# Softmax sums from a column of ones in the stage ahead of the expert slots

## The chip, the cores and the metric

One NeuronCore of one Trainium2 chip runs the whole program. The metric is the device time of one execution in microseconds (us), the median of the runs shown; differences are of a few us in some 650.

## The reference

Windowed attention, whose output rows are then sent through a mixture of eight experts, one expert for each token:

```
q, k, v: (8, 8, 576, 64) float32         # batch, heads, sequence, head_dim
scores = q k^T / 8, only where 0 <= i - j < 64, else -1e9
scores -= max;  attn = exp(scores);  attn /= (sum(attn) + 1e-9)
x = (attn v) as (4608, 512)              # token rows, heads side by side
logits = x w_gate + modality_bias[modality_id];  e_idx = argmax(logits)
gate_w = the chosen expert's softmax probability
out[rows of e] = gate_w * (relu(x w1[e]) w2[e])   # w1: 512x1024, w2: 1024x512
```

## The kernel before, in words

The 4608 token rows are 36 pairs of two 64-row blocks, 128 rows each. A block of queries sees its own block of keys and the one before. The main loop (L947 on) has one step s for each pair, and four more; each step holds work of several pairs, one stage each: scores and minima of pair s, transposes of the probabilities of pair s-1, values of pair s-2, router logits of pair s-3. Two pairs form a group G, for which queries and keys are turned (transposed on TensorE, copied out of PSUM by `heads_out`) in the steps before: the keys in the even step, the queries in the odd one, each in two halves of four heads.

The order of the instructions on every engine is that of the program text (`manual_schedule`); no scheduler changes it. An engine works through its queue in order, and waits where the next instruction's input is not there.

In one step, for pair s: TensorE computes `scores` into two PSUM banks sp0 and sp1; VectorE takes the row minima of the negated, masked scores head by head (`minima`, tile ss, mn); ScalarE takes the exponentials head by head (`exps`) and with `accum_out` also their sums, read by an instruction of its own (ACTIVATION_READ_ACCUMULATOR); a step later TensorE turns the probabilities (`probs_t`) and ScalarE copies them to pT; GpSimd adds 1e-9 to the sums (`sums`, tile rs). The values come in as vo (128 rows, heads, 64). The keys of a row's window lie in its own block and the one before, so a second tile ve holds the values exchanged: GpSimd copies the pair's lower half into ve's lower rows and VectorE the neighbour pair's upper half into ve's upper rows (`swap_v`, L503 and L502; "the neighbour copy" below is the latter). `values` multiplies pT with ve and vo into one PSUM bank av, 32 matmuls in the trace's count of two for each product; `values_out` takes the reciprocal of rs and multiplies (tile xa). `x_t` turns xa, `logits` and `route1` to `route3` choose the expert and compute each row's place, and GpSimd scatters xa's rows to a scratch tensor in DRAM, sorted by expert (L716).

All turns ask `turn_bank` for a PSUM bank: before step 11 there are five (two of tp, and em, y0, y1, which the slots use later), from step 11 on the two of tp.

Beside that, expert weights come in as pieces of 128x512, which are split into a high part (ScalarE, L111) and a low part (VectorE, L116), one piece a step.

From step FIRST = 12 on, pieces of expert slots stand between the parts of a step: matmuls of 256 sorted rows with one expert's weights, in three products of high and low parts (L279, L301). After the last step only slots remain. A wait is chosen by the order: the first slot's rows are loaded in step 11 (`fetch`).

The names and lines that matter: `turn_bank` L474, `load_v` L483, `swap_v` L495, `heads_out` L534, `exps` L583, `sums` L601, `values` L607, `values_out` L619, and the step's body from L947.

Of the kernel before, what the change touches and what calls it, by code (L numbers as in the profile page):

```python
# [19 lines left out]
P = 128  # L20
W64 = 64
# [5 lines left out]
def tile_window_attn_moe(  # L27
# [447 lines left out]
    def turn_bank(s):  # L475

        i = n_tp[0]
        n_tp[0] += 1
        if s < FIRST - 1 and i % 5 > 1:
            return ps_m.tile([P, 512], F32, name=("em", "y0", "y1")[i % 5 - 2])  # L480
        return ps_t.tile([P, 512], F32, name="tp")

    def load_v(p):  # L483
        t = work.tile([P, H, D], F32, name="vo", bufs=3)
        vo[p] = t
        g0, g1 = 2 * p, 2 * p + 1
        if g0 // BPB == g1 // BPB:
            s0 = (g0 % BPB) * W64
            nc.sync.dma_start(out=t, in_=v_v[g0 // BPB, s0:s0 + P])
        else:  # L490
            for i, g in enumerate((g0, g1)):
                s0 = (g % BPB) * W64
                nc.sync.dma_start(out=t[i * W64:(i + 1) * W64], in_=v_v[g // BPB, s0:s0 + W64])

    def swap_v(p):  # L495

        e = work.tile([P, H, D], F32, name="ve", bufs=2)
        ve[p] = e
        if p == 0:
            nc.gpsimd.memset(e[W64:P], 0.0)  # L500
        else:
            nc.vector.tensor_copy(out=e[W64:P], in_=vo[p - 1][W64:P])  # L502
        nc.gpsimd.tensor_copy(out=e[0:W64], in_=vo[p][0:W64])  # L503

    def new_qk(G, nm):
        if G in AHEAD:
# [94 lines left out]
    def sums(p):  # L601
        sm = st[p, "s"][2]
        rs = st[p, "rs"] = small.tile([P, H], F32, name="rs")
        nc.gpsimd.tensor_scalar(out=rs, in0=sm, scalar1=1e-9, scalar2=None, op0=ALU.add)


    def values(p):  # L607
        st.pop((p, "s"))
        av = st[p, "av"] = ps_a.tile([P, H, D], F32, name="av")
        for u in range(H):  # L610
            a, hp = divmod(u, HP)
            pT = st[p, "p", a]
            for c in range(2):
                i = hp * P + c * W64
                nc.tensor.matmul(  # L615
                    out=av[c * W64:(c + 1) * W64, 2 * hp + a], lhsT=pT[:, i:i + W64],
                    rhs=(vo if c else ve)[p][:, 2 * hp + a, :], start=True, stop=True)

    def values_out(p):  # L619
        rs = st.pop((p, "rs"))  # L620
        nc.vector.reciprocal(out=rs, in_=rs)
        xa = st[p, "xa"] = xas[p % XBUF]
        nc.vector.tensor_tensor(  # L623
            out=xa[:, 0:DM].rearrange("p (h d) -> p h d", d=D), in0=st.pop((p, "av")),
            in1=rs[:, :, None].broadcast_to([P, H, D]), op=ALU.mult)
# [24 lines left out]
    def route1(G):  # L650

        lg = st.pop((G, "lg"))
        oh = chosen[G]
        lm = small.tile([P, GB], F32, name="lm")
        ex = small.tile(sh3, F32, name="ex")
        wn = small.tile(sh3, F32, name="wn")
        wm = small.tile([P, GB], F32, name="wm")
# [187 lines left out]
    for h in range(2):  # L845
        rows = slice(h * W64, (h + 1) * W64)
        own = slice(h * W64, (h + 1) * W64)
        before = slice((1 - h) * W64, (2 - h) * W64)
        for m in range(3):
            nc.gpsimd.affine_select(  # L850
                out=masks[rows, m, own], in_=masks[rows, m, own],
                compare_op=ALU.is_ge, fill=NEG, base=0,
                pattern=[[-1, W64]], channel_multiplier=1)
            if m == h + 1:
                nc.gpsimd.memset(masks[rows, m, before], NEG)
            else:
# [89 lines left out]
    for s in range(NPR + 4):  # L946
# [201 lines left out]
    while next(it, "end") != "end":  # L1148
# [6 lines left out]
        for n in range(RAWS):  # L1155
            if n < len(swaps) and n == len(ahead) and swaps[n][0] <= t + RAWS:
                _, buf, x, c = swaps[n]
                tick(ready_a - issued[0], table=True)
                nm = ("vo", "ss", "pT")[n_raw[0] % RAWS % 3]
                n_raw[0] += 1  # L1160
                sh = [P, H, D] if nm == "vo" else [P, HP, P] if nm == "ss" else [P, HP * P]
                raw = work.tile(sh, F32, name=nm, bufs=2 if nm == "pT" else 3)
                if nm != "pT":
                    raw = raw.rearrange("p a b -> p (a b)")
# [130 lines left out]
```

## Time and profile before

| what | us |
|---|---|
| median of three runs | 648.55 |
| lowest and highest | 647.55 and 649.33 |
| profiled execution | 648.28 |
| its span | 646.4 |
| busy in the span: TensorE | 620.0 |
| VectorE | 367.7 |
| ScalarE | 299.4 |
| GpSimd | 137.4 |

The profile shows one execution. Busy time of an engine is the time in which one of its instructions runs; of TensorE it is a modelled time, since matmuls overlap. Instructions on VectorE and ScalarE overlap a little too: the next one starts before the one ahead has written its last element, so what an instruction costs its engine is read from its start to the next one's start. "PE" is TensorE, "DVE" VectorE, "ACT" ScalarE, "POOL" GpSimd, "SP" the queue that starts most transfers. In the page's 40 slices of 16 us TensorE is at six to eight tenths in the first six, and at nine or more in nearly all that follow: the first part is the attention alone, steps 0 to 11, up to about 88 us.

### The profile page before, as it was taken

Reading aid. Unit: us, or ns where it says so; the run is one execution under the profiler, and the core shown is the slowest. Engines: PE = TensorE matmul, PEld = TensorE weight load, DVE = VectorE, ACT = ScalarE, POOL = GpSimd, SP = SyncE. Lnnn points to the kernel's source line nnn. Section 1 sums busy time; section 2 is a strip of 40 time slices with the busy share of each in tenths; the row PEclk is TensorE's granted clock in tenths of the full one; section 3 lists DMA queues with packets and bytes.
Section 4 is the critical chain, followed back from the end, with each engine's and each line's share of the span. In section 5 each row is a group of like instructions: output and inputs, shape, how many; then the busy total and the mean of one; then the engine's idle time right before and its main releaser. Section 6 shows DMA issues by size and latency. Waiting matters only on the chain.

```text
span 646.4 us, 17286 instructions
## 1 busy us (share of the span) xinstructions
PE 620.0 (96%) x6508; PEld 554.6 (86%) x6509; DVE 367.7 (57%) x1494; ACT 299.4 (46%) x932; POOL 137.4 (21%) x314
## 2 busy tenths in 40 slices
PE   6888889999999999999999999999999999999996
PEld 4677779898989888889998898899898999989986
DVE  2889967777767686766655365122214524757611
ACT  2789875756565646555544111111113513555411
POOL 4315330232142212320322220011011101101102
PEclk9999989999999999999999999999999999999999
DMA  9988975764876754553412124421041732677300
GB/s 164 195 186 216 212 197 132 196 161 120 181 171 153 159 144 103 144 133 82 132 51 83 50 99 171 157 67 66 23 173 45 236 113 85 218 247 227 120 1 36
DMA packets 138885, 88.07 MB, mean 136 GB/s; under 512 B 116746, under 2 KB 116784, under 8 KB 138672
## 3 DMA queue, kind: packets, MB, share of 16 engines
q1 hardware_dynamic: 130112, 67.44, 42.2%
q0 software_dynamic: 5856, 18.92, 7.8%
q10 hardware_dynamic: 2832, 0.59, 0.6%
q8 instruction: 52, 0.85, 0.6%
q14 instruction: 33, 0.27, 0.2%
HBM read 67.49 MB, written 23.91 MB: 141 GB/s over the span
## 4 chain that ended last, share of the span: by engine, by line
PE 50%; DVE 0%; ACT 0%; issue 0%; POOL 0%; POOLq 0%; ACTq 0%
PE y L301 22%; PE em L279 12%; PE sp L279 10%; PE tp L439 1%; PE y L352 1%; PE av L615 1%; PE em L254 1%; PE tp L254 1%; PE sp L327 0%; PE em L327 0%; PE tp L640 0%; PE sp L563 0%; DVE xa L623 0%; ACT ss L589 0%; DVE hl L288 0%
## 5 line engine op out<-in xcount | busy, mean ns | idle before, releaser
L301 PE MATMUL y<-Whi,hh 128*128 128x512 f32 x288 | 118.7, 412 | 0.0
L301 PE MATMUL y<-Wlo,hh 128*128 128x512 f32 x288 | 112.9, 392 | 0.0
L301 PE MATMUL y<-Whi,hl 128*128 128x512 f32 x288 | 112.8, 392 | 0.0
L589 ACT ACTIVATE ss<-ss,mn 128x128 f32<-128x128 f32 x288 | 112.5, 397 | 0.0
L279 PE MATMUL em<-xh,Whi 128*128 128x256 f32 x400 | 103.5, 293 | 1.2 <-ACT xh L192 0.7
L279 PE MATMUL em<-xh,Wlo 128*128 128x256 f32 x400 | 98.5, 280 | 0.0
L288 DVE SCALAR_TENSOR_TENSOR hl<-em,hh 128x512 fp32r<-128x512 f32 x50 | 34.5, 690 | 92.9 <-ACT hh L287 91.3
L312 POOL DMA_INDIRECT out_dram<-y,id x36 | 37.3, 1036 | 224.6 <-DVE y L309 145.9
L279 PEld LDWEIGHTS em<-xh,Whi 128*128 128x128 f32 x400 | 75.9, 190 | 2.6 <-ACT xh L192 0.9
L279 PEld LDWEIGHTS em<-xh,Wlo 128*128 128x128 f32 x400 | 75.8, 190 | 0.9
L287 ACT ACTIVATE hh<-em 128x512 fp32r<-128x512 f32 x50 | 29.6, 592 | 93.3 <-PE em L279 89.4
L577 DVE CUSTOM_DVE_ANT_0 ss<-sp,masks 128x128 f32<-128x128 f32 x288 | 63.5, 286 | 13.4 <-PE sp L563 13.4
L598 ACT COPY pT<-tp 128x512 f32<-128x512 f32 x58 | 32.2, 589 | 78.0 <-PE tp L439 78.0
L301 PEld LDWEIGHTS y<-Whi,hl 128*128 128x128 f32 x288 | 54.1, 188 | 12.3
L279 PE MATMUL em<-xl,Whi 128*128 128x256 f32 x400 | 63.4, 281 | 0.0
L301 PEld LDWEIGHTS y<-Whi,hh 128*128 128x128 f32 x288 | 54.1, 188 | 7.5
L301 PEld LDWEIGHTS y<-Wlo,hh 128*128 128x128 f32 x288 | 54.3, 188 | 7.1
L589 ACT ACTIVATION_READ_ACCUMULATOR ss<-ss,mn 128x1 f32 x288 | 55.8, 194 | 0.0
L716 POOL DMA_INDIRECT xs_scratch<-xa,idx x36 | 36.3, 1007 | 89.1 <-DVE lm L659 26.9
L279 PEld LDWEIGHTS em<-xl,Whi 128*128 128x128 f32 x400 | 54.2, 189 | 0.0
L288 DVE SCALAR_TENSOR_TENSOR hl<-sp,hh 128x512 fp32r<-128x512 f32 x22 | 15.2, 692 | 61.1 <-ACT hh L287 61.1
L615 PEld LDWEIGHTS av<-ve,pT 128*64 128x64 f32 x576 | 36.4, 138 | 15.2 <-issue 7.4
(242 smaller groups left out, 1243.6 us busy)
## 6 DMA issues: line engine op xcount, KB each, us to landing
xt<-xs_scratch SPq DMA_DIRECT2D x18, 514.0 KB, 4.0
vo<-in_v_dram SPq DMA_DIRECT2D x32, 256.0 KB, 4.1
y<-in_moe_w_dram SPq DMA_DIRECT2D x32, 256.0 KB, 4.0
vo<-in_moe_w_dram SPq DMA_DIRECT2D x24, 256.0 KB, 3.5
ss<-in_moe_w_dram SPq DMA_DIRECT2D x24, 256.0 KB, 3.8
qk<-in_k_dram SPq DMA_DIRECT2D x18, 256.0 KB, 5.5
qk<-in_q_dram SPq DMA_DIRECT2D x18, 256.0 KB, 4.9
xs_scratch<-xs_scratch SPq DMA_DIRECT2D x8, 514.0 KB, 6.0
```

The lines of the kernel that those rows point to most:

```text
L254: nc.tensor.transpose(out=tp[:, n * P:(n + 1) * P].bitcast(F32R), in_=xt[:, t, c * P:(c + 1) * P].bitcast(F32R), identity=ident_r)
L279: nc.tensor.matmul(out=hb[:, i * TP:(i + 1) * TP], lhsT=w[buf][:, c0:c0 + P], rhs=x[:, c * TP:(c + 1) * TP], start=(n == 0), stop=(n == le ...
L287: nc.scalar.activation(out=hh, in_=hb, func=AF.Relu),
L288: nc.vector.scalar_tensor_tensor(out=hl, in0=hb, scalar=0.0, in1=hh.bitcast(F32), op0=ALU.max, op1=ALU.subtract)))
L301: nc.tensor.matmul(out=sl["y", t], lhsT=h[:, i * TP + t * P:i * TP + (t + 1) * P], rhs=w[buf][:, c0:c0 + DM], start=(k == 0 and n == 0), s ...
L312: ins = nc.gpsimd.indirect_dma_start(out=out, out_offset=bass.IndirectOffsetOnAxis(ap=sl["id"][:, t:t + 1], axis=0), in_=y, in_offset=None ...
L352: nc.tensor.matmul(out=yp[:, cols], lhsT=sl["h", n][lo][:, c * P:(c + 1) * P], rhs=w[buf][:, c0 + cols.start:c0 + cols.stop], start=(m == ...
L577: nc.vector.tensor_tensor_reduce(out=ss[a][:, hp, :], in0=sp[a][:, hp * P:(hp + 1) * P], in1=mask, scale=-1.0 / 8.0, scalar=3.0e38, op0=AL ...
L589: nc.scalar.activation(out=ss[a][:, hp, :], in_=ss[a][:, hp, :], func=AF.Exp, bias=mn[:, h:h + 1], scale=-1.0, accum_out=sm[:, h:h + 1])
L598: nc.scalar.copy(out=pT, in_=pp)
L615: nc.tensor.matmul(out=av[c * W64:(c + 1) * W64, 2 * hp + a], lhsT=pT[:, i:i + W64], rhs=(vo if c else ve)[p][:, 2 * hp + a, :], start=Tru ...
L716: ins = nc.gpsimd.indirect_dma_start(out=xs, out_offset=bass.IndirectOffsetOnAxis(ap=idx[:, j:j + 1], axis=0), in_=xg[j], in_offset=None)
```

## The change

It concerns the pairs p < 12 (FIRST), whose work stands mostly ahead of the slots.

- The value tiles vo and ve get a 65th column for each head, set to one at the start. The exponentials no longer give sums (`accum_out` is None for p < 12). `values` takes 65 columns, so column 64 of each head's product is the sum of the probabilities. Eight heads of 65 columns don't fit one PSUM bank, so four heads go to av and four to y1.
- `values_out` adds 1e-9 to the two columns of sums on VectorE (two instructions of 128x4), takes the reciprocal as before, and multiplies in two parts of 128x256. GpSimd's add goes.
- `turn_bank` has four banks instead of five before step 11, without y1.
- The neighbour copy moves from VectorE, behind the minima, to ScalarE, at the start of the step (`swap_upper`). For p >= 12 it stays on VectorE, and also moves to the step's start.
- The second half of the queries' copy moves from VectorE to ScalarE in the steps before 12, as the second half of the keys' was.
- vo and ve become fixed tiles instead of ones drawn from a pool; two small tiles share names with others (wm with lm, tgt with wn).

```diff
-        if s < FIRST - 1 and i % 5 > 1:
-            return ps_m.tile([P, 512], F32, name=("em", "y0", "y1")[i % 5 - 2])
+        if s < FIRST - 1 and i % 4 > 1:
+            return ps_m.tile([P, 512], F32, name=("em", "y0")[i % 4 - 2])
...
     def swap_v(p):
-        e = work.tile([P, H, D], F32, name="ve", bufs=2)
-        ve[p] = e
+        e = ve[p]
         if p == 0:
             nc.gpsimd.memset(e[W64:P], 0.0)
-        else:
-            nc.vector.tensor_copy(out=e[W64:P], in_=vo[p - 1][W64:P])
         nc.gpsimd.tensor_copy(out=e[0:W64], in_=vo[p][0:W64])
+
+    def swap_upper(p):
+        ve[p] = ves[p % 2]
+        if p > 0:
+            copy = nc.scalar.copy if p < FIRST else nc.vector.tensor_copy
+            copy(out=ve[p][W64:P], in_=vo[p - 1][W64:P])
...
-                bias=mn[:, h:h + 1], scale=-1.0, accum_out=sm[:, h:h + 1])
+                bias=mn[:, h:h + 1], scale=-1.0, accum_out=sm[:, h:h + 1] if p >= FIRST else None)
...
-        av = st[p, "av"] = ps_a.tile([P, H, D], F32, name="av")
+        av = [ps_a.tile([P, 512], F32, name="av")]
+        if p < FIRST:
+            av.append(ps_m.tile([P, 512], F32, name="y1"))
+            av = [t[:, 0:HP * (D + 1)].rearrange("p (h d) -> p h d", h=HP) for t in av]
...
+        if p < FIRST:
+            for i in range(2):
+                nc.vector.tensor_scalar(
+                    out=rs[:, i * HP:(i + 1) * HP], in0=av[i][:, :, D], scalar1=1e-9, scalar2=None, op0=ALU.add)
         nc.vector.reciprocal(out=rs, in_=rs)
...
+        if 1 <= s <= NPR:
+            swap_upper(s - 1)
...
-            heads_out(tp, G, *heads[1], nc.scalar.copy if heads[1] == K1 else nc.vector.tensor_copy)
+            heads_out(tp, G, *heads[1], nc.scalar.copy if heads[1] == K1 or s < FIRST else nc.vector.tensor_copy)
```

On VectorE, in step 7 and the start of step 8 (ve is the neighbour copy's target, qT the queries', tgt or wn the rows' places, Wlo a weight piece, rs the sums, lg the logits), before:

```order
L502 COPY ve<-vo 64x512
L539 COPY qT<-tp 128x2x2x128
L697 TENSOR_TENSOR tgt<-tp,ebase 128x16
L539 COPY qT<-em 128x2x2x128
L702 TENSOR_REDUCE se<-ex 128x2
...
L116 TENSOR_TENSOR Wlo_66<-y,Whi_65 128x512
L621 RECIPROCAL rs<-rs 128x8
L623 TENSOR_TENSOR xa_102<-av,rs 128x512
L645 TENSOR_TENSOR lg<-y_1245,bias_sel 128x8
```

and after:

```order
L545 COPY qT<-tp 128x2x2x128
L720 TENSOR_TENSOR wn<-em,ebase 128x16
L725 TENSOR_REDUCE se<-ex 128x2
...
L116 TENSOR_TENSOR Wlo_66<-y,Whi_65 128x512
L641 TENSOR_SCALAR rs<-av 128x4
L641 TENSOR_SCALAR rs<-y_1239 128x4
L643 RECIPROCAL rs<-rs 128x8
L646 TENSOR_TENSOR xa_102<-av,rs 128x256
L646 TENSOR_TENSOR xa_102<-y_1239,rs 128x256
L668 TENSOR_TENSOR lg<-tp,bias_sel 128x8
```

Two copies are gone from the step; two adds and a second multiplication have come.

On ScalarE, in step 7 (Whi is a weight piece, pT the probabilities, xaT the turned rows, the exponentials are the ones on ss), before:

```order
L111 CAST Whi_65<-y 128x512
L598 COPY pT<-em 128x512
L598 COPY pT<-y_1161 128x512
L589 ACTIVATE ss,sm<-ss,mn 128x128 x2
L632 COPY xaT<-y_1172 128x512
L589 ACTIVATE ss,sm<-ss,mn 128x128 x6
L111 CAST Whi_65<-y 128x512
```

and after:

```order
L111 CAST Whi_65<-y 128x512
L509 COPY ve_110<-vo_109 64x520
L604 COPY pT<-em 128x512
L604 COPY pT<-y_1174 128x512
L595 ACTIVATE ss<-ss,mn 128x128 x2
L655 COPY xaT<-tp 128x512
L595 ACTIVATE ss<-ss,mn 128x128 x6
L545 COPY qT<-y_1212 128x2x2x128
L111 CAST Whi_65<-y 128x512
```

The neighbour copy stands ahead of the probabilities' copies, the second query copy behind the exponentials, and the exponentials write no sums.

## Rows read from the trace of the kernel before

**Rows 1.** Busy us (instructions) by stretch: PE, PEld, DVE, ACT, POOL; clock, DMA share, GB/s
```profile
60.00:75.00 15.00, 12.58 (x225) 11.02 (x225) 14.45 (x82) 14.33 (x55) 7.41 (x13) 1.00 0.96 219
...
105.00:120.00 15.00, 15.00 (x229) 13.24 (x228) 12.50 (x60) 9.19 (x31) 3.62 (x7) 1.00 0.52 138
```

**Rows 2.** Timeline of VectorE: start us, duration us, engine, line, operation [idle before <-releaser]
```profile
18.97 0.29 DVE L577 CUSTOM_DVE_ANT_0 ss<-sp,masks 128x128 f32<-128x128 f32 x1 [2.20 <-PE sp L563]
...
48.73 0.28 DVE L577 CUSTOM_DVE_ANT_0 ss<-sp,masks 128x128 f32<-128x128 f32 x1
...
56.47 0.42 DVE L502 COPY ve<-vo 64x512 f32<-64x512 f32 x1
56.93 0.69 DVE L539 COPY qT<-tp 128x512 f32<-128x512 f32 x1
...
57.74 0.68 DVE L539 COPY qT<-em 128x512 f32<-128x512 f32 x1
58.34 0.16 DVE L702 TENSOR_REDUCE se<-ex 128x2 f32<-128x16 f32 x1
...
58.88 0.15 DVE L728 CAST idx<-dst 128x2 int32<-128x2 f32 x1
...
59.54 0.20 DVE L621 RECIPROCAL rs<-rs 128x8 f32<-128x8 f32 x1
59.82 0.69 DVE L623 TENSOR_TENSOR xa<-av,rs 128x512 f32<-128x512 f32 x1
60.43 0.15 DVE L645 TENSOR_TENSOR lg<-y,bias_sel 128x8 f32<-128x8 f32 x1
60.50 0.28 DVE L577 CUSTOM_DVE_ANT_0 ss<-sp,masks 128x128 f32<-128x128 f32 x1
...
66.32 0.28 DVE L577 CUSTOM_DVE_ANT_0 ss<-sp,masks 128x128 f32<-128x128 f32 x1
...
83.46 0.69 DVE L539 COPY qT<-tp 128x512 f32<-128x512 f32 x1 [0.67 <-PE tp L439]
```

**Rows 3.** Waits from 15 to 95 us: engine, line, awaited: total us, times, longest us
```profile
DVE ss L577 <- PE sp L563: 4.0, 3, 2.2
```

**Rows 4.** Timeline of ScalarE, step 0 and steps 6 and 7
```profile
14.72 0.41 ACT L589 ACTIVATE ss<-ss,mn 128x128 f32<-128x128 f32 x1
...
17.81 0.60 ACT L539 COPY kT<-tp 128x512 f32<-128x512 f32 x1
...
49.06 0.59 ACT L598 COPY pT<-em 128x512 f32<-128x512 f32 x1
49.54 0.41 ACT L589 ACTIVATE ss<-ss,mn 128x128 f32<-128x128 f32 x1
49.85 0.20 ACT L589 ACTIVATION_READ_ACCUMULATOR ss<-ss,mn 128x1 f32 x1
...
51.96 0.21 ACT L663 ACTIVATE ex<-lg 128x16 f32<-128x16 f32 x1
52.06 0.39 ACT L589 ACTIVATE ss<-ss,mn 128x128 f32<-128x128 f32 x1
...
55.24 0.59 ACT L598 COPY pT<-em 128x512 f32<-128x512 f32 x1 [0.89 <-PE em L439]
```

**Rows 5.** Timeline of TensorE, steps 7, 8, 9 and 11
```profile
54.49 0.66 PE L439 MATMUL em<-ident_r,ss 128*128 128x128 f32 x4
...
59.65 0.66 PE L439 MATMUL y<-ident_r,ss 128*128 128x128 f32 x4
...
63.24 0.27 PE L615 MATMUL av<-ve,pT 128*64 128x64 f32 x1 [1.15 <-DVE lg L660]
...
79.41 0.65 PE L439 MATMUL tp<-ident_r,ss 128*128 128x128 f32 x4 [0.94 <-DVE lg L645]
```

**Rows 6.** Timeline of GpSimd: its half of ve behind two scatters
```profile
62.33 0.86 POOL L503 COPY ve<-vo 64x512 f32<-64x512 f32 x1
```

**Rows 7.** Busy us by stretch, columns as in the first group, at the first slot
```profile
92.00:94.00 2.00, 2.00 (x11) 2.00 (x11) 1.51 (x6) 0.86 (x5) 0.77 (x1) 0.50 0.64 182
```

More of the change, by code (lines that the diff above doesn't have):

```diff
@@ L459, in tile_window_attn_moe @@
     first_oh = small.tile([P, GB + 1, E], BF16, name="oh", bufs=3)
+    vos = [att.tile([P, H, D + 1], F32, name=f"vo{i}") for i in range(3)]
+    ves = [att.tile([P, H, D + 1], F32, name=f"ve{i}") for i in range(2)]
     v_v = v.rearrange("b h s d -> b s h d")
@@ L478, in turn_bank @@
         n_tp[0] += 1
-        if s < FIRST - 1 and i % 5 > 1:
-            return ps_m.tile([P, 512], F32, name=("em", "y0", "y1")[i % 5 - 2])
+        if s < FIRST - 1 and i % 4 > 1:
+            return ps_m.tile([P, 512], F32, name=("em", "y0")[i % 4 - 2])
         return ps_t.tile([P, 512], F32, name="tp")
     def load_v(p):
-        t = work.tile([P, H, D], F32, name="vo", bufs=3)
-        vo[p] = t
+        t = vo[p] = vos[p % 3]
         g0, g1 = 2 * p, 2 * p + 1
@@ L488, in load_v @@
             s0 = (g0 % BPB) * W64
-            nc.sync.dma_start(out=t, in_=v_v[g0 // BPB, s0:s0 + P])
+            nc.sync.dma_start(out=t[:, :, 0:D], in_=v_v[g0 // BPB, s0:s0 + P])
         else:
@@ L603, in sums @@
         rs = st[p, "rs"] = small.tile([P, H], F32, name="rs")
-        nc.gpsimd.tensor_scalar(out=rs, in0=sm, scalar1=1e-9, scalar2=None, op0=ALU.add)
+        if p >= FIRST:
+            nc.gpsimd.tensor_scalar(out=rs, in0=sm, scalar1=1e-9, scalar2=None, op0=ALU.add)
     def values(p):
         st.pop((p, "s"))
-        av = st[p, "av"] = ps_a.tile([P, H, D], F32, name="av")
+        av = [ps_a.tile([P, 512], F32, name="av")]
+        if p < FIRST:
+            av.append(ps_m.tile([P, 512], F32, name="y1"))
+            av = [t[:, 0:HP * (D + 1)].rearrange("p (h d) -> p h d", h=HP) for t in av]
+        else:
+            st[p, "whole"] = av[0].rearrange("p (h d) -> p h d", d=D)
+            av = [st[p, "whole"][:, i * HP:(i + 1) * HP] for i in range(2)]
+        st[p, "av"] = av
+        cols = slice(0, D + 1 if p < FIRST else D)
         for u in range(H):
             a, hp = divmod(u, HP)
+            h = 2 * hp + a
             pT = st[p, "p", a]
@@ L615, in values @@
                 nc.tensor.matmul(
-                    out=av[c * W64:(c + 1) * W64, 2 * hp + a], lhsT=pT[:, i:i + W64],
-                    rhs=(vo if c else ve)[p][:, 2 * hp + a, :], start=True, stop=True)
+                    out=av[h // HP][c * W64:(c + 1) * W64, h % HP], lhsT=pT[:, i:i + W64],
+                    rhs=(vo if c else ve)[p][:, h, cols], start=True, stop=True)
     def values_out(p):
         rs = st.pop((p, "rs"))
-        nc.vector.reciprocal(out=rs, in_=rs)
[L622 to L625, printed above, removed]
+        av = st.pop((p, "av"))
+        xa = st[p, "xa"] = xas[p % XBUF]
+        if p < FIRST:
+            for i in range(2):
+                nc.vector.tensor_scalar(
+                    out=rs[:, i * HP:(i + 1) * HP], in0=av[i][:, :, D], scalar1=1e-9, scalar2=None, op0=ALU.add)
+        nc.vector.reciprocal(out=rs, in_=rs)
+        parts = [(av[i][:, :, 0:D], i * HP, HP) for i in range(2)] if p < FIRST else [(st.pop((p, "whole")), 0, H)]
+        for part, h0, n in parts:
+            nc.vector.tensor_tensor(
+                out=xa[:, h0 * D:(h0 + n) * D].rearrange("p (h d) -> p h d", d=D), in0=part,
+                in1=rs[:, h0:h0 + n, None].broadcast_to([P, n, D]), op=ALU.mult)
     def x_t(p, xp):
@@ L656, in route1 @@
         wn = small.tile(sh3, F32, name="wn")
-        wm = small.tile([P, GB], F32, name="wm")
+        wm = small.tile([P, GB], F32, name="lm")
         nxt = chosen[G + 1] = small.tile([P, GB + 1, E], BF16, name="oh", bufs=3)
@@ L695, in route3 @@
         xg = [st.pop((GB * G + j, "xa")) for j in range(GB)]
-        tgt = small.tile(sh3, F32, name="tgt")
+        tgt = small.tile(sh3, F32, name="wn")
         nc.vector.tensor_tensor(
@@ L860, in tile_window_attn_moe @@
                     pattern=[[1, W64]], channel_multiplier=-1)
+    for t in vos + ves:
+        nc.gpsimd.memset(t[:, :, D:], 1.0)
     nc.gpsimd.memset(first_oh, 0.0)
@@ L1159, in tile_window_attn_moe @@
                 nm = ("vo", "ss", "pT")[n_raw[0] % RAWS % 3]
+                if nm == "vo":
+                    raw = vos[n_raw[0] % RAWS // 3].rearrange("p h d -> p (h d)")[:, 0:WCH]
+                else:
+                    raw = work.tile([P, HP, P] if nm == "ss" else [P, HP * P], F32, name=nm, bufs=2 if nm == "pT" else 3)
+                if nm == "ss":
+                    raw = raw.rearrange("p a b -> p (a b)")
                 n_raw[0] += 1
[L1161 to L1164, printed above, removed]
                 ahead.append((load_piece(raw, ea[x], c), buf, c))
```

2 lines of the change are left out of this document (1 added, 1 removed).

## The prediction

> **What bounds the kernel now.** I read the table of busy time by stretch first, to find where the change works. From 105 us on TensorE is busy all the time (15.00 of 15 us), while in the attention stage it has gaps (12.58 of 15) and VectorE (14.45) and ScalarE (14.33) have almost none [rows 1]. What comes behind is TensorE's own work in a fixed order, so a microsecond won before step 12 is a microsecond won at the end, and one won on another engine later is worth nothing.
>
> Next, VectorE in order of time, since it has the fewest gaps. M(s) is the start of the first minimum of step s. From M(6) at 48.73 to M(8) at 60.50 are 11.77 us, and its instructions follow one another without a wait [rows 2]. Up to M(12), 2.77 us after the last row of the group, it waits for scores three times: 4.0 in total, of them 2.20 ahead of M(1) at 18.97 and 1.8 ahead of M(4) and M(5); and 0.67 for a turn in step 11 [rows 2, 3]. So it is the bound of steps 6 to 10. The scores wait for ScalarE: its copy of the keys stands behind eight exponentials (14.72 to 17.81, 0.386 us each), and M(1) follows [rows 4]. ScalarE itself waits only 0.89 us in the pair of steps 6 and 7 [rows 4], so some 10.9 of 11.77 are its own work. TensorE needs 5.16 from one step's transposes to the next where nothing holds it (54.49 to 59.65) [rows 5]: not far behind the other two.
>
> **The change part by part, on VectorE.** All sums run from M(1) to M(12), in us.
>
> Removed: the neighbour copy, 0.46 from its start to the next instruction (56.47 to 56.93), in steps 2 to 11: 10 x 0.46 = 4.6. The second query copy, 0.60 (57.74 to 58.34), in the odd steps 1 to 11: 6 x 0.60 = 3.6 [rows 2].
>
> Added, in 10 of the steps: two adds of 128x4 and a second multiplication. The trace has no such add. The nearest row is the logits' add on 128x8 out of PSUM, which lets the next instruction start 0.07 later (60.43 to 60.50); the nearest dependent pair is reciprocal to multiplication, 0.28 (59.54 to 59.82) [rows 2]. The two adds are independent and the reciprocal needs both: 0.07 + 0.20 = 0.27, with 0.15 as the low bound and 2 x 0.28 as the high one. The multiplication holds the engine 0.61 (59.82 to 60.43) [rows 2]; halved, the second part pays the start again, about 0.07 by the small add, bounds 0 and 0.15. Together 0.34 a step, bounds 0.15 and 0.71: 3.4, from 1.5 to 7.1. I take the middle because the small add is the row of the same kind.
>
> Waits: 1.8 + 0.67 = 2.5 go if the scores come earlier [rows 2, 3]. The start: M(1) waits for the keys behind eight exponentials; without the accumulator reads these end 8 x 0.19 = 1.5 earlier (price below), and M(1) with them.
>
> **On ScalarE.** An exponential's accumulator read starts 0.31 after it (49.54 to 49.85), the next exponential at 0.386 [rows 4]. Without the read the pitch is not in the trace. Its bounds are 0.10 (the 16-wide exponential, 51.96 to 52.06) and 0.31; a copy of 512 columns takes 0.48 (49.06 to 49.54) [rows 4], and in proportion between 16 and 512 columns 128 come to 0.19, which I take. A pair of steps loses 16 x 0.196 = 3.1 and gains two neighbour copies and one query copy at 0.48: 1.4. 10.9 - 3.1 + 1.4 = 9.2: ScalarE stops being a bound. The neighbour copy stands ahead of the transposed probabilities, for which ScalarE waited 0.89 [rows 4]; there it is hidden every other step. If that cover is gone it costs up to 0.48 a step, but on an engine with 1.5 to spare. Behind it are queued the probabilities' copies and all exponentials; it waits only for values loaded and read a step before.
>
> A 512-wide copy holds ScalarE 0.48 and the accumulator read comes at 0.31, as said [rows 4]. [...]
>
> **TensorE and the queues.** The values' 32 matmuls of a step stream 65 columns in place of 64; I cost that at nothing, at most 0.1 us a step, beside VectorE's work. The turns have four banks for five. In step 11, where there are only two, a turn waits 0.94 for VectorE [rows 5]; with four the bank's last reader is four turns back, and I take nothing, with 0.94 a step as the far end and nothing to gain, since a bank less frees no one. GpSimd loses its sums for the first twelve pairs. Its half of the neighbour copy still stands behind two scatters: it starts at 62.33 and takes 0.86, and TensorE's values start at 63.24, 0.05 after it [rows 5, 6]. From the index that starts the scatters to M(9), 58.88 to 66.32, are 7.44 [rows 2], by this way and by VectorE's alike; VectorE's becomes 7.44 - 0.46 + 2 x 0.34 = 7.66, so this chain stays just below it. The load of the values waited for VectorE's copy and now waits for ScalarE's, half a step sooner, so it and the loads behind it on SP go out earlier. The transfers are busy 0.96 of this stretch [rows 1]: that they keep up rests on this lead.
>
> **The sum.** VectorE alone: -1.5 - 4.6 - 3.6 + 3.4 - 2.5 = -8.8. But where VectorE needs less than TensorE's 5.16, TensorE sets the step. From M(3) to M(4), 5.13 with 0.57 of the waits, VectorE would need 5.13 - 0.57 - 0.46 - 0.60 + 0.34 = 3.84, so 1.3 come back, and steps 4, 5 and 7 give back another 0.3. In step 11, with two banks for its turns, I let TensorE take back 0.8, nearly the 0.94 above. That is +2.4: -6.4. A pair of steps is then 11.77 - 0.92 - 0.60 + 0.68 = 10.9 for VectorE, at least 10.3 for TensorE and 9.2 for ScalarE; where three engines are so close, handovers cost a little, and I give back 0.6, an estimate without a row of its own. So -5.8: 648.28 - 5.8 = 642.5 on the scale of the profiled execution. The median of the runs is 0.27 above it: 642.8.
>
> Beyond step 12 the neighbour copy stands ahead of the multiplication on VectorE; TensorE has work then [rows 1], and I cost it at nothing. If that cover failed, 0.46 a step.
>
> **Rivals.**
> 1. Half the gain: ScalarE stays near the bound. If an exponential without its read holds the engine 0.31, a pair is 10.9 - 16 x 0.076 + 1.4 = 11.1, plus some 0.3 of waits for transposes: 0.3 to 0.6 below 11.77, in five and a half pairs 1.7 to 3.3, and 0.6 at the start: 645.5. For it: the read starts no sooner than at 0.31. Against it: the 512-wide copies at 0.48. The same time would come from late transfers. Chance 0.20.
> 2. No change, 648.4: VectorE's additions cost their upper bound, 7.1, and eat what it lost, with what TensorE takes back. Against it: only a dependent pair costs 0.28, and there is one such pair more, not two. 0.05.
> 3. Slower, 652: the fifth bank. If each step's turns wait 0.94 for a reader, as in step 11 [rows 5], eleven steps lose 10.3 against the 5.8 won. It decides from 0.53 a step. Against it: the reader is four turns back, more than half a step. 0.08.
> 4. The change doesn't do what it says: the exponential without its read keeps 0.386. Then ScalarE's pair is 10.9 + 1.4 = 12.3, 0.5 over the present one, 2.8 in all: 651. Against it: the read has rows of its own [rows 4]. 0.03.
> 5. [...] 0.04.
>
> **How the numbers follow.** The forecast has 0.60, its own spread 640.5 to 645. The range leaves out rivals 2 to 4 and a tail below: 639.6 to 647.2. A measurement of this kernel tells 0.3% (2 us) from no change. Faster: forecast, rival 1 but for its weakest part, and 5: 0.83. Within: rival 2 and that part, 0.06. Slower: rivals 3 and 4, 0.11.
>
> **What would show it.** Right: no accumulator reads on ScalarE ahead of step 12 and exponentials 0.19 apart; M(8) - M(6) near 10.9; M(1) near 17.5; the reciprocal 0.27 after the first add; the first slot's matmuls some 6 us sooner, and from there to the end the same distance as before. Wrong: waits on VectorE for scores in steps 6 to 10, which were not there; turns that wait for a bank's reader; values that wait for GpSimd or for a load; a longer stretch at half the clock.

## The result, and the profile after

The changed kernel takes 651.32 us (median of 9 runs, 650.43 to 651.51) against 648.45 for the one before: ratio 1.0043, interval 1.003 to 1.0056. It is slower by 2.9 us, where 5.8 less was forecast. The profiled execution has a span of 649.6 us against 646.4. Ratios here and below compare fast executions; only the kernel with GpSimd's copy (median 658.50 of six, ratio 1.0112) had slow ones, two.

With M(s) the start of the first minimum of step s on VectorE, as in the prediction, the 3.2 us between the spans split like this (us; after minus before):

| stretch | before | after | difference |
|---|---|---|---|
| start to M(1) | 18.97 | 18.69 | -0.28 |
| M(1) to M(12): attention stage | 67.26 | 65.10 | -2.16 |
| M(12) to M(13): first slot begins | 12.58 | 13.76 | +1.18 |
| M(13) to M(35): slots beside attention | 237.04 | 240.50 | +3.46 |
| M(35) to the last run of expert products (L352) in the chain that ended last | 299.73 | 300.08 | +0.35 |
| from there to the end | 10.82 | 11.47 | +0.65 |

So two things went wrong in two stages. Up to M(12) the gain came out at 2.44 us, where 5.8 was forecast, and the slots beside attention, which were to cost nothing, lost 3.46. Nor does the gain lie where the prediction took its pair of steps: from M(6) to M(8) the kernel after is 0.18 slower, and it wins 0.94 ahead of M(6) and 1.40 behind M(8).

The busy time by stretch of the kernel after, columns as in [rows 1]:

```profile
60.00:75.00 15.00, 13.60 (x272) 12.19 (x274) 13.06 (x85) 14.52 (x39) 4.76 (x10) 1.00 0.87 208
105.00:120.00 15.00, 15.00 (x233) 13.42 (x232) 12.93 (x69) 8.63 (x28) 3.40 (x7) 1.00 0.70 188
...
200.00:250.00 50.00, 48.66 (x641) 43.42 (x643) 34.41 (x158) 28.95 (x103) 14.00 (x28) 1.00 0.65 158
```

In 60 to 75 us VectorE fell from 14.45 to 13.06, as it should. ScalarE did not fall: 14.33 before [rows 1], 14.52 now. In 200 to 250 TensorE has 1.34 us of gaps; in the kernel before it had 0.75:

```profile
200.00:250.00 50.00, 49.25 (x659) 44.09 (x660) 35.08 (x160) 29.09 (x104) 14.05 (x30) 1.00 0.65 159
```

VectorE of the kernel after, in order of time, the same view as [rows 2] (start, duration, operation, idle before it and its releaser):

```profile
18.69 0.29 DVE L583 CUSTOM_DVE_ANT_0 ss<-sp,masks 128x128 f32<-128x128 f32 x1 [1.67 <-PE sp L569]
...
57.33 0.15 DVE L641 TENSOR_SCALAR rs<-av 128x4 f32<-128x4 f32 x1
57.40 0.15 DVE L641 TENSOR_SCALAR rs<-y 128x4 f32<-128x4 f32 x1
57.59 0.20 DVE L643 RECIPROCAL rs<-rs 128x8 f32<-128x8 f32 x1
57.83 0.42 DVE L646 TENSOR_TENSOR xa<-av,rs 128x256 f32<-128x256 f32 x1
58.17 0.41 DVE L646 TENSOR_TENSOR xa<-y,rs 128x256 f32<-128x256 f32 x1
58.50 0.15 DVE L668 TENSOR_TENSOR lg<-tp,bias_sel 128x8 f32<-128x8 f32 x1
59.46 0.29 DVE L583 CUSTOM_DVE_ANT_0 ss<-sp,masks 128x128 f32<-128x128 f32 x1 [0.81 <-PE sp L569]
```

The added work is priced rightly: 0.26 from the first add to the reciprocal (0.27 forecast), and 0.67 for the two multiplications (0.61 + 0.07). But the minima now wait for scores in nine steps, 4 to 10 among them. VectorE's waits, in the view of [rows 3], went from 4.0 us in 3 times to

```profile
DVE ss L583 <- PE sp L569: 8.0, 9, 1.7
```

and those scores wait for ScalarE's copies of keys and queries. ScalarE in order of time, steps 6 and 7 of the kernel after, the same view as [rows 4] (a row with x2 or x6 joins so many in a run):

```profile
47.27 0.62 ACT L509 COPY ve<-vo 64x520 f32<-64x520 f32 x1
48.13 1.08 ACT L604 COPY pT<-tp 128x512 f32<-128x512 f32 x2 [0.24 <-PE tp L439]
...
52.17 0.59 ACT L545 COPY kT<-tp 128x512 f32<-128x512 f32 x1
...
53.30 0.62 ACT L509 COPY ve<-vo 64x520 f32<-64x520 f32 x1
54.17 0.59 ACT L604 COPY pT<-em 128x512 f32<-128x512 f32 x1 [0.24 <-PE em L439]
54.65 0.59 ACT L604 COPY pT<-y 128x512 f32<-128x512 f32 x1
55.27 0.69 ACT L595 ACTIVATE ss<-ss,mn 128x128 f32<-128x128 f32 x2
...
56.34 1.86 ACT L595 ACTIVATE ss<-ss,mn 128x128 f32<-128x128 f32 x6
58.10 0.59 ACT L545 COPY qT<-y 128x512 f32<-128x512 f32 x1
58.58 0.61 ACT L111 CAST Whi<-y 128x512 fp32r<-128x512 f32 x1
59.22 0.62 ACT L509 COPY ve<-vo 64x520 f32<-64x520 f32 x1
```

Six exponentials without their reads take 56.34 to 58.10: a pitch of 0.293, not the 0.19 of the forecast. The neighbour copy holds the engine 0.62, not 0.48. From 47.27 to 59.22, one pair of steps, ScalarE waits 2 x 0.24 of 11.95 us, and a pair of steps is 11.95 where it was 11.77.

ScalarE sets the pace now, together with TensorE: its wait is not time to spare. TensorE, step 7:

```profile
52.82 0.67 PE L569 MATMUL sp<-kT,qT 64*64 64x128 f32 x16 [0.94 <-ACT kT L545]
53.42 0.66 PE L439 MATMUL em<-ident_r,ss 128*128 128x128 f32 x4
```

ScalarE copies the keys at 52.17, the scores wait for that copy, the turn of the probabilities follows them, and ScalarE's copy of that turn starts at 54.17. The key copy, a weight piece and the neighbour copy fill 1.75 of these 2.00 us. The next step has the same (58.10 to 60.09), and so had the kernel before without the neighbour copy there (53.22 to 55.24).

In the slot phase the view to read is the list of TensorE's waits. Kernel before and kernel after, 95 to 385 us (awaited: total us, times, longest):

```profile
PE tp L439 <- DVE lg L645: 1.3, 3, 0.7
```

```profile
PE tp L439 <- DVE lg L668: 4.9, 6, 1.3
```

These are waits of the turns of probabilities for VectorE's addition to the logits. In the kernel after they come in steps 13, 17, 21, 25, 29 and 33, the last five 0.71, 0.71, 1.34, 0.68 and 1.09 us; the kernel before waited in 25 (0.75), 33 (0.17) and 36 (0.37) alone. The 3.6 us more from M(13) to M(35) account for the 3.46 lost there. One such place, step 25: VectorE and TensorE of the kernel after,

```profile
227.68 0.73 DVE L309 TENSOR_SCALAR y<-y,gate 128x512 f32<-128x512 f32 x1
228.44 0.43 DVE L509 COPY ve<-vo 64x520 f32<-64x520 f32 x1
228.90 0.20 DVE L643 RECIPROCAL rs<-rs 128x8 f32<-128x8 f32 x1
229.19 0.69 DVE L646 TENSOR_TENSOR xa<-av,rs 128x512 f32<-128x512 f32 x1
229.80 0.16 DVE L668 TENSOR_TENSOR lg<-tp,bias_sel 128x8 f32<-128x8 f32 x1
```

```profile
228.01 0.66 PE L439 MATMUL tp<-ident_r,ss 128*128 128x128 f32 x4
230.01 0.66 PE L439 MATMUL tp<-ident_r,ss 128*128 128x128 f32 x4 [1.34 <-DVE lg L668]
```

in step 17, where the kernel before doesn't wait,

```profile
141.60 0.66 PE L439 MATMUL tp<-ident_r,ss 128*128 128x128 f32 x4 [0.71 <-DVE lg L668]
```

and TensorE of the kernel before:

```profile
228.09 0.66 PE L439 MATMUL tp<-ident_r,ss 128*128 128x128 f32 x4
229.50 0.66 PE L439 MATMUL tp<-ident_r,ss 128*128 128x128 f32 x4 [0.75 <-DVE lg L645]
```

From step 11 on there are two turn banks. The logits take one, the first turn of probabilities the other, and the second turn needs the first bank again, which VectorE's addition of the logits (`lg`) must have read. That addition now stands behind the neighbour copy. TensorE waits where VectorE comes late from a slot's work (L309), which stands there in steps 17, 21, 25, 29 and 33. In 25 and 33 the copy lengthens a wait; in the others the addition had come just in time, and now doesn't. From the first of these turns to the next expert product, steps 17, 21, 25 and 29 lost 0.58 to 0.60 us each and step 33 lost 0.93.

### The profile page after: what moved, and what is told of

It reads as the page before. It is cut to its first block, busy times and chain, and to the rows that moved or that the text cites. A ratio compares the mean times of both kernels' runs of the same rounds, so it can differ in the third digit from the quotient of the medians.

```text
span 649.6 us, 17205 instructions
## 1 busy us (share of the span) xinstructions
PE 622.5 (96%) x6509; PEld 555.8 (86%) x6509; DVE 360.0 (55%) x1513; ACT 301.6 (46%) x853; POOL 132.4 (20%) x307
## 4 chain that ended last, share of the span: by engine, by line
PE 56%; ACT 0%; DVE 0%; issue 0%; POOL 0%; POOLq 0%; ACTq 0%
PE y L301 24%; PE em L279 14%; PE sp L279 9%; PE tp L439 3%; PE av L631 1%; PE sp L569 1%; PE y L352 1%; PE em L254 1%; PE tp L254 1%; PE tp L663 1%; PE sp L327 0%; PE em L327 0%; DVE xa L646 0%; ACT ss L595 0%; DVE hl L288 0%
## 5 line engine op out<-in xcount | busy, mean ns | idle before, releaser
L595 ACT ACTIVATE ss<-ss,mn 128x128 f32<-128x128 f32 x288 | 105.8, 394 | 0.3
L604 ACT COPY pT<-tp 128x512 f32<-128x512 f32 x61 | 34.2, 589 | 80.9 <-PE tp L439 80.9
L583 DVE CUSTOM_DVE_ANT_0 ss<-sp,masks 128x128 f32<-128x128 f32 x288 | 63.5, 285 | 14.2 <-PE sp L569 14.0
L569 PE MATMUL sp<-kT,qT 64*64 64x128 f32 x1152 | 43.7, 285 | 7.6 <-ACT kT L545 4.0
L287 ACT ACTIVATE hh<-sp 128x512 fp32r<-128x512 f32 x22 | 13.1, 597 | 76.6 <-PE sp L279 76.6
```

The lines of the kernel that those rows point to most:

```text
L287: nc.scalar.activation(out=hh, in_=hb, func=AF.Relu),
L569: nc.tensor.matmul(out=sp[a][c * W64:(c + 1) * W64, hp * P:(hp + 1) * P], lhsT=qT[rows, hp, g + c, :], rhs=kT[rows, hp, win[c], :], start= ...
L583: nc.vector.tensor_tensor_reduce(out=ss[a][:, hp, :], in0=sp[a][:, hp * P:(hp + 1) * P], in1=mask, scale=-1.0 / 8.0, scalar=3.0e38, op0=AL ...
L595: nc.scalar.activation(out=ss[a][:, hp, :], in_=ss[a][:, hp, :], func=AF.Exp, bias=mn[:, h:h + 1], scale=-1.0, accum_out=sm[:, h:h + 1] if ...
L604: nc.scalar.copy(out=pT, in_=pp)
```

## The experiments

Theory: (A) in the attention stage ScalarE became the bound, by the pitch of the exponentials and the two copies it was given; in the slot phase the moved copy delays the logits' addition. Rivals: (B) the slot phase loses through the late start of step 13 or the bank order; (C, D) in the attention stage a chain through the engines sets the pace, not ScalarE's sum; the four banks. In all, M(1) to M(12) is read for the attention stage and M(13) to M(35) for the slots. The stretch between them depends on whether TensorE's clock fell there in the one execution that was profiled (last section), so totals of single executions are not compared.

Each ratio is to runs of the kernel before made beside that kernel (medians 648.15 to 648.45).

| kernel | time us | ratio to before, interval | M(1)-M(12) | M(13)-M(35) |
|---|---|---|---|---|
| before (profiled) | 648.45 | 1 | 67.26 | 237.04 |
| after | 651.32 | 1.0043, 1.003-1.0056 | 65.10 | 240.50 |
| copy at its old place in the slot phase | 646.79 | 0.9976, 0.9966-0.9986 | 65.11 | 236.91 |
| before, with the move alone | 652.79 | 1.0075, 1.0051-1.0098 | 67.16 | 240.23 |
| the same again, another chip | 652.98 | 1.0074, 1.0058-1.0091 | 67.24 | 240.24 |
| copy behind the logits' addition | 645.82 | 0.9962, 0.9948-0.9975 | 65.10 | 236.35 |
| old place; neighbour copy on VectorE | 646.65 | 0.9981, 0.9965-0.9997 | 66.53 | 237.28 |
| column of ones only | 649.33 | 1.0018, 1.0007-1.0029 | 69.26 | 236.90 |
| old place; Q1 copy on VectorE | 642.71 | 0.9916, 0.9894-0.9938 | 63.10 | 236.84 |
| old place; neighbour copy on GpSimd | 658.50 | 1.0112, 1.0061-1.0163 | 77.45 | 237.27 |
| old place; accumulator reads kept | 656.18 | 1.0117, 1.0094-1.014 | 74.91 | 236.85 |
| before, with four banks | 648.03 | 0.9997, 0.9985-1.0009 | 67.47 | 236.99 |
| Q1 on VectorE, without the adds | 642.82 | 0.9912, 0.9896-0.9928 | 62.38 | 236.90 |
| both mends | 643.18 | 0.9928, 0.9909-0.9947 | 63.71 | 236.37 |

**The moved copy taken back, and moved alone.** In the changed kernel, with the copy for p >= FIRST (pair 12, so step 13) in `swap_v` again:

```
 def swap_upper(p):
-    if p > 0:
-        copy = nc.scalar.copy if p < FIRST else nc.vector.tensor_copy
-        copy(out=ve[p][W64:P], in_=vo[p - 1][W64:P])
+    if p > 0 and not (p >= FIRST):
+        nc.scalar.copy(out=ve[p][W64:P], in_=vo[p - 1][W64:P])
 def swap_v(p):
+    if p > 0 and (p >= FIRST):
+        nc.vector.tensor_copy(out=e[W64:P], in_=vo[p - 1][W64:P])
```

> The changed kernel, but from step 13 on (first slot running) the neighbour's copy stands on VectorE where it stood before, behind the minima instead of ahead of the sums' and values' work. Theory A (the move of that copy delays the logits' addition, for which TensorE waits between the two turns of probabilities): the 4.6 us that the slot phase loses between M12 (-2.4 against before) and the end of TensorE's chain (+2.6) go, and what stays is the gain of the attention stage: 645.5 to 647 us, and TensorE's wait for the logits' addition falls from 4.9 us in 95 to 385 us to near the 1.3 of before. Rival B (the slot phase loses through the late start of step 13 or through the changed bank order, which this kernel keeps): 650 to 651.5, with the waits as in the changed kernel.

And the kernel before, with only that move (shown is the call; `swap_v` leaves the copy out for these pairs):

```
+        if FIRST < s <= NPR:
+            swap_upper(s - 1)      # VectorE's copy, taken out of swap_v
         if 2 <= s < NPR + 2:
             values(s - 2)
```

> The kernel before, with only the neighbour's copy of the pairs from 12 on moved to the start of its step on VectorE; no column of ones, no copy on ScalarE. Theory A: this alone costs 3.5 to 5.6 us, 652 to 654 us, and up to step 12 nothing differs. Rival B: 648.5 within 0.7 us, since VectorE is not the bound there.

> The kernel before with only the move of the neighbour's copy to the start of the step from step 13 on, a second time on another chip: 652 to 654 us as the first time (652.8, +4.4), or, if the first was a matter of the chip, 648.5.

All three came out as theory A has it: 646.8, and 652.8 and 653.0. The move alone costs 4.4 to 4.6 us, and 3.2 of it lie in M(13) to M(35). With the copy at its old place that stretch is 236.91 (before 237.04) and TensorE's wait is again

```profile
PE tp L439 <- DVE lg L669: 1.3, 3, 0.7
```

**Which instruction was in the way.** The changed kernel, with the copy a few instructions later, still ahead of the minima:

```
-        if 1 <= s <= NPR:
+        if 1 <= s <= FIRST:
             swap_upper(s - 1)
         ...
             logits(s - 3, turn_bank(s))
+        if FIRST < s <= NPR:
+            swap_upper(s - 1)
         if s < NPR:
             scores(s)
```

> The changed kernel, with one thing moved: from step 13 on VectorE's copy of the neighbour's values stands behind the logits' addition and ahead of the scores' minima, in place of the step's start; the Q1 copy and the neighbour's copy of the attention stage are as in the change. Theory A1 (the loss is the wait of the second turn of probabilities for the logits' addition): M13 to M35 falls back from 240.5 to about 237, time 646.5 to 648. Theory A2 (the loss is that the minima, and so the exponentials, start 0.5 us later in every step, wherever the copy stands ahead of them): M13 to M35 stays near 240, time 650.5 to 651.5.

645.82, 0.7 under A1's range, and M(13) to M(35) 236.35: it is the logits' addition (A1), not the minima (A2), which start as late as with the copy at the step's start. The same place of step 25 on VectorE and on TensorE:

```profile
227.03 0.15 DVE L668 TENSOR_TENSOR lg<-tp,bias_sel 128x8 f32<-128x8 f32 x1
227.21 0.52 DVE L509 COPY ve<-vo 64x520 f32<-64x520 f32 x1
227.76 0.29 DVE L583 CUSTOM_DVE_ANT_0 ss<-sp,masks 128x128 f32<-128x128 f32 x1
```

```profile
227.24 0.66 PE L439 MATMUL tp<-ident_r,ss 128*128 128x128 f32 x4 [0.75 <-DVE lg L668]
```

The wait is back to 0.75, as in the kernel before.

**Two copies, two engines.** With the slot phase mended, the three other ways to place the two copies of the attention stage. The neighbour copy on VectorE, in `swap_v`, for all p (`swap_upper` then copies nothing):

```
 def swap_v(p):
-    if p > 0 and (p >= FIRST):
+    if p > 0:
         nc.vector.tensor_copy(out=e[W64:P], in_=vo[p - 1][W64:P])
```

> As the run with the copy at its old place in the slot phase, and in the attention stage too the neighbour's copy is on VectorE behind the minima; the column of ones and the Q1 copy on ScalarE stay. Theory A (ScalarE is the bound of the attention stage after the change; the copy of 64 x 520 costs it 0.62 us a step, VectorE 0.46): ScalarE falls from 5.8 to 5.2 us a step, VectorE rises from 4.2 to 4.6 busy plus its waits, and a step from 5.9 to 5.5 to 5.7: 643 to 645.5 us. Rival C (the step's chain through scores, minima, exponentials and copies sets the pace, not ScalarE's sum): no gain over the run with the copy on ScalarE, 646 to 647.

That, and the Q1 copy on VectorE as well; then the Q1 copy alone:

```
-  heads_out(tp, G, *heads[1], nc.scalar.copy if heads[1] == K1 or s < FIRST else nc.vector.tensor_copy)
+  heads_out(tp, G, *heads[1], nc.scalar.copy if heads[1] == K1 else nc.vector.tensor_copy)
```

> The column of ones alone: sums from it while no slot runs, exponentials without the read of the accumulator; both copies (the neighbour's behind the minima, Q1) on VectorE as in the kernel before. Theory A: ScalarE is relieved of 8 x 0.093 = 0.74 us a step, VectorE pays two additions of together 0.34; VectorE was the busier engine before, so between no change and 10 x 0.34 = 3.4 more: 648.5 to 652. Rival C (ScalarE's read held the chain): 646 to 647.5, all of the change's gain from this part alone.

> As the run with the slot phase's copy at its old place (646.8 us; M1 to M12 65.1 us), but the Q1 copy is on VectorE again in every second step; the column of ones and the neighbour's copy on ScalarE stay. Theory A (ScalarE sets the pace there, and VectorE waits 0.6 to 1.2 us a step for scores, which take up the copy of 0.6): M1 to M12 falls by 5 x 0.48 = 2.4 us, 644.4. Theory D (the two engines hand over to each other, and what the Q1 copy takes from VectorE just ahead of the sums and values is on the chain): M1 to M12 rises by 1 to 2.7 us, since the same copy moved the other way between the runs with the column of ones alone (69.3) and with it (66.5): 647.5 to 649.5.

| M(1) to M(12), us | Q1 copy on VectorE | Q1 copy on ScalarE |
|---|---|---|
| neighbour copy on VectorE | 69.26 | 66.53 |
| neighbour copy on ScalarE | 63.10 | 65.11 |

The busy time of 60 to 75 us (columns as in [rows 1]), kernel by kernel. Ones only:

```profile
60.00:75.00 15.00, 12.48 (x224) 11.14 (x223) 14.52 (x87) 12.10 (x33) 6.28 (x10) 1.00 0.86 200
```

The copy at its old place (both of the attention stage's copies on ScalarE):

```profile
60.00:75.00 15.00, 13.60 (x281) 12.15 (x279) 13.00 (x84) 14.61 (x40) 4.37 (x9) 1.00 0.89 213
```

Q1 copy on VectorE, neighbour copy on ScalarE:

```profile
60.00:75.00 15.00, 13.08 (x264) 11.37 (x259) 14.20 (x87) 14.15 (x37) 3.43 (x6) 1.00 1.01 220
```

With nothing moved VectorE is full (14.52) and ScalarE has 2.9 to spare; with both moved ScalarE is full (14.61) and VectorE has 2.0 to spare; with the neighbour copy alone moved both are at 14.2. The Q1 copy gains 2.7 us when it goes to ScalarE in the first case and loses 2.0 in the second. That sign change is what a bound that passes from one engine to another gives, and a fixed chain through VectorE (D) doesn't. The third kernel, 642.7, is faster than before by 5.4 us, and 1.7 better than A's 644.4; M(1) to M(12) fell by 2.0 for the 2.4 of A. The medians of the two kernels are 4.1 apart; what lies outside the stage is only in part placed (0.45 of it ahead of M(1)).

With the Q1 copy left on ScalarE, taking the neighbour copy off it gave nothing: 646.65, in rival C's 646 to 647 and not in A's 643 to 645.5. There the copy's time became a wait for the turned probabilities, 0.89 where it had been 0.24:

```profile
54.25 0.59 ACT L605 COPY pT<-em 128x512 f32<-128x512 f32 x1 [0.89 <-PE em L439]
```

So C holds in this much: the copy of keys or queries, the scores and the turn are a chain back to ScalarE, and the neighbour copy is done in time that ScalarE would else spend waiting for it. VectorE's minima hardly wait in that kernel either (once from 40 to 75 us, 0.5), so which of the two sets its 11.75 us a pair is not separated.

**The accumulator reads put back** (the column of ones still gives the sums; the reads' sums are left unused):

```
-  accum_out=sm[:, h:h + 1] if p >= FIRST else None)
+  accum_out=sm[:, h:h + 1])
```

> As the run with the slot phase's copy at its old place, but the exponentials of the attention stage keep their sums (and so the read of the accumulator, pitch 0.386 in place of 0.293), which nothing uses; the sums still come from the column of ones. Theory A (ScalarE is the bound after the change): 8 x 0.093 = 0.74 us a step, so 5.5 to 8 us over 11 steps: 652 to 655. Rival D (a chain through several engines, with ScalarE's sum under it): 0 to 3 us, 647 to 650.

656.2, 1.2 over the top of what A expected and far from D's 647 to 650; M(1) to M(12) grew by 9.8 us, 1.6 more than 11 x 0.74; in part of that stage TensorE ran below its full clock (granted 0.93 in 15 to 40 us, 0.97 in 40 to 60 and 0.92 in 60 to 75), which may be the rest. So the exponentials' pitch is in what sets the pace, as A and a chain through ScalarE both have it. The exponential, its read and the next start on ScalarE:

```profile
57.63 0.39 ACT L596 ACTIVATE ss<-ss,mn 128x128 f32<-128x128 f32 x1
57.92 0.20 ACT L596 ACTIVATION_READ_ACCUMULATOR ss<-ss,mn 128x1 f32 x1
58.01 0.39 ACT L596 ACTIVATE ss<-ss,mn 128x128 f32<-128x128 f32 x1
```

The read adds 0.09 to a pitch of 0.29; its own 0.20 mostly lies beside the exponential.

**GpSimd as a third place**, in `swap_upper` for p < FIRST:

```
-        nc.scalar.copy(out=ve[p][W64:P], in_=vo[p - 1][W64:P])
+        nc.gpsimd.tensor_copy(out=ve[p][W64:P], in_=vo[p - 1][W64:P])
```

> As the run with the slot phase's copy at its old place, but in the attention stage the neighbour's copy (64 x 520) is on GpSimd at the step's start, neither on ScalarE nor on VectorE. GpSimd's copy of the other half lasts 0.62 to 0.66 us there. Theory A (ScalarE is the bound, 0.62 us a step of it is this copy): M1 to M12 falls by 3 to 6 us from 65.1, 641 to 644 us. Rival D (chain, not the sum): under 1 us, 646 to 647. Rival F (GpSimd's copy comes late, behind the wait of its scatter, and the values' matrix products wait for it): slower than the run with the copy on ScalarE, 647.5 to 652.

Rival F's way, and slower than its 652: 658.5, from 650.4 to 662.4. In four steps the values wait for GpSimd, 11.6 us in all on TensorE and at most 4.2. One of them, and GpSimd's rows ahead of it:

```profile
54.00 0.27 PE L632 MATMUL av<-ve,pT 128*64 128x65 f32 x1 [3.69 <-POOL ve L505]
```

```profile
48.17 0.96 POOL L740 DMA_INDIRECT xs_scratch<-xa,idx  x1 [0.28 <-POOL xa L739]
52.66 0.62 POOL L510 COPY ve<-vo 64x520 f32<-64x520 f32 x1 [3.53 <-DMA xs_scratch<-xa,idx]
53.33 0.61 POOL L505 COPY ve<-vo 64x520 f32<-64x520 f32 x1
```

GpSimd has the time, but not then. What held its copy for 3.53 us is inferred by the profile and was not tested. The granted clock was lower here too (0.91 in 40 to 60 us, 0.89 in 60 to 75), so not all of the loss need be these waits.

**Four banks alone**, in the kernel before:

```
-        if s < FIRST - 1 and i % 5 > 1:
-            return ps_m.tile([P, 512], F32, name=("em", "y0", "y1")[i % 5 - 2])
+        if s < FIRST - 1 and i % 4 > 1:
+            return ps_m.tile([P, 512], F32, name=("em", "y0")[i % 4 - 2])
```

> The kernel before, with turns cycling over four PSUM banks instead of five up to step 10 and nothing else: the change's own bank count. Theory: no change, within 0.7 us of 648.4, since the exits of these banks wait little. The prediction's rival of the four banks: turns wait for the exit of the bank four turns back, 3 to 4 us more, 651 to 652.

648.03, 0.9997: the prediction's rival of the fifth bank is out.

**Two more steps from the fastest.** Without the additions of 1e-9 in the attention stage:

```
-                nc.vector.tensor_scalar(out=rs[:, i * HP:(i + 1) * HP], in0=av[i][:, :, D],
-                    scalar1=1e-9, scalar2=None, op0=ALU.add)
-        nc.vector.reciprocal(out=rs, in_=rs)
+                nc.vector.reciprocal(out=rs[:, i * HP:(i + 1) * HP], in_=av[i][:, :, D])
+        else:
+            nc.vector.reciprocal(out=rs, in_=rs)
```

> As the run with the slot phase's copy at its old place and the Q1 copy on VectorE (642.7 us), without the two additions of 1e-9 in the attention stage: the reciprocals, two of 4 columns, read the sums from PSUM. A sum of exponentials that holds an exp(0) is at least 1, where 1e-9 is below float32's last place. VectorE issues one instruction fewer in a step (0.15 and 0.15 and 0.20 become about 0.2 and 0.2, and one wait of two instructions on each other goes). Theory A (VectorE and ScalarE are both at 95% and more there): 0.1 to 0.3 us a step, so 1 to 3 us: 640 to 642. Rival (ScalarE alone sets the pace now): no change, 642.3 to 643.2.

And the two mends together, the diff of the copy behind the logits' addition with that of the Q1 copy:

> The changed kernel with its two costly parts mended: from step 13 on the neighbour's copy behind the logits' addition (as in the run so named, M13 to M35 236.4), and the Q1 copy on VectorE in all steps (as in the run so named, M1 to M12 63.1). Theory A (the two mends act in stages that follow each other, so they add up): 8.6 us under the changed kernel from the one by M1 to M12 and 5.5 to 6 from the other give 651.3 - 2.0 - 5.5 = 643.8 at most, and with M13 to M35 0.5 shorter than with the copy behind the minima 642.2: 641.5 to 643. Rival: the shorter attention stage lets the slot phase start in another state, and the 0.5 is lost: 643 to 644.

642.82 and 643.18: neither differs from 642.71 by more than such runs tell apart. The first is in the range of its rival (ScalarE alone sets the pace) and outside A's 640 to 642; the second is just over A's 643. The adds are worth 0.7 us in M(1) to M(12) at most. In the last one M(13) to M(35) kept its 0.5 us (236.37), while M(1) to M(12) was 0.6 longer with the same text of that stage (63.71 and 63.10), most of it between M(1) and M(2): 6.93 for 6.53. The cause of that is open.

## Why the prediction was wrong

**The step that failed on size: "An exponential without its read".** The step "in proportion between 16 and 512 columns 128 come to 0.19, which I take", with bounds of 0.10 and 0.31, measured 0.293. The proportion ran between a row of 16 columns and a copy out of PSUM, another operation with another source. For a pair of steps that is 16 x 0.10 = 1.6 us that ScalarE did not lose. With the neighbour copy at 0.64 from start to start for 0.48 (0.3 a pair), the 9.2 forecast becomes 11.1; 11.47 of 11.95 were measured as ScalarE's own (11.95 less its two waits of 0.24). Of the last 0.4, 0.28 are the first exponential of each step, which starts 0.62 after the second copy of probabilities (54.65 to 55.27) for 0.48 before [rows 4]. It does so in the kernels with the neighbour copy on ScalarE; why is open. The other 0.48 of the 11.95 are the two waits of the chain through TensorE. The prediction set ScalarE's own work alone against VectorE's, and so took such waits for spare time.

**So rival 1 held for this stage**, place and cause: "ScalarE stays near the bound". It forecast 645.5; with the slot phase mended the kernel takes 646.8 and 645.8. That the times agree is partly luck: the rival had a pair of steps 0.3 to 0.6 below 11.77, and it measured 0.18 above, while the gain came in the other steps. The two copies that the change gave to ScalarE were one too many: the 2 x 2 table shows that the neighbour copy alone is worth 6.2 us there (69.26 to 63.10), and both together 4.2.

**The step that failed on mechanism: "Beyond step 12 ... I cost it at nothing".** TensorE was busy 15.00 of 15 us [rows 1], and I read it as cover for all that follows 105 us. That stretch holds none of the waits: it shows 15.00 in the kernel after too, while 200 to 250 us has gaps of 0.75 and 1.34 us, the waits of step 25. And a busy TensorE is cover only where it waits for none of what VectorE does behind the copy. The kernel before had the wait already (0.75 us in step 25, 1.3 in three waits of the list), and in three more steps the logits' addition had no time to spare. The fallback, 0.46 a step, would have been 10.1 over these 22 steps; measured are 3.2 to 3.5 us, nearly all of it in the five steps where VectorE is late from a slot's work. A mechanism of this kind with its price belonged among the rivals as the slower case. The two that stood there as slower, four banks and a read that costs nothing, are refuted by 648.03 and by the pitch of 0.293.

**What held.** VectorE's terms: the column of ones adds 0.70 to a pair of steps with VectorE as the bound (12.47 against 11.77; 0.68 forecast), and with the Q1 copy gone the pair is 11.75 (11.85 by the forecast's terms), where VectorE may not be the only bound.

**What else did not.** The start follows from the same term: 8 reads of 0.09, 0.74, where 8 x 0.19 = 1.5 were forecast; from M(0) to M(1) the kernels without the reads took 0.4 to 0.8 less than before. TensorE's 2.4 to give back can't be read from this kernel, where ScalarE's chain stops the steps first. The 0.6 given back for handovers was an estimate, and no run shows it as a term of its own; what the kernel after shows between engines are the waits of 0.24 for the turns.

**Not settled.** M(12) to M(13) grew by 1.18. With the copy behind the logits' addition it is 13.37 for 13.76, and the move alone adds 0.3 to 0.55 to the kernel before; the rest is not separated from the clock. The last 0.65 us is the end of the last scatter: it is issued at 642.63 in the kernel before and at 645.17 in the one after, 1.3 after VectorE's last instruction starts in both, and the span ends 3.8 and 4.4 later. The kernels with the new tiles of values show this longer end (11.35 with the column of ones only), all but that with GpSimd's copy (10.87); no run tells why.

## What to carry to other kernels

Before a copy is moved to the start of a step on an engine that "has time", list what stands behind it there and look for that in the busy engine's waits, over the whole phase: one stretch at 15.00 of 15 us says nothing of a wait that comes every fourth step, some 44 us apart. When two engines are both near the bound, move one item and read both again; the second item may gain with one place of the first and lose with the other. Take the duration of an instruction without its accumulator read from a like instruction with the same source and size, not by proportion from another, which gave 0.19 here for a measured 0.293.

## What the runs showed of the hardware

- An exponential of 128x128 in SBUF has a pitch of 0.293 us on ScalarE, with the accumulator read 0.386. A 512-wide copy out of PSUM lets the next instruction start 0.48 after it (0.62 ahead of the exponentials where the neighbour copy is on ScalarE), a 520-wide copy of 64 rows in SBUF 0.64 to 0.65 after it.
- TensorE's clock, at the first slot. In the kernel after, two stretches (columns as in [rows 1]):

```profile
88.00:90.00 2.00, 1.19 (x7) 0.99 (x8) 1.97 (x6) 2.00 (x10) 0.46 (x1) 0.96 1.28 149
90.00:92.00 2.00, 2.00 (x12) 2.00 (x11) 1.50 (x6) 0.77 (x5) 0.25 (x1) 0.50 0.93 277
```

With the copy at its old place, the same two:

```profile
88.00:90.00 2.00, 1.32 (x11) 1.11 (x11) 1.97 (x5) 2.00 (x10) 0.91 (x1) 1.00 1.30 157
90.00:92.00 2.00, 2.00 (x20) 2.00 (x18) 1.08 (x4) 1.52 (x5) 0.78 (x1) 1.00 1.00 271
```

In the first of these two the granted clock fell to 0.50, behind 2 us in which TensorE was busy 1.19; in the second it stayed at 1.00, behind 1.32. Such a pair makes no rule: with both mends the clock stayed at 1.00 behind 1.21 us busy (86 to 88 us), and with the column of ones only behind 1.17 (90 to 92 us). A stretch at a lower granted clock like that of [rows 7] (0.50 there) came between M(12) and M(13) in eight of the fourteen profiled executions, before and after among them, and M(12) to M(13) was 12.58 to 13.76 there. In the other six the clock stayed up, and it was 11.08 to 11.71. So one profiled execution of such a kernel can flatter it by over 1 us, and the stretches on either side of it are the ones to compare.
